# Attention feeding a routed expert layer: three moves in the order of the GpSimd queue

## The chip, the core and the metric

The kernel runs on one core of a Trainium2 chip. The core has a matrix engine (PE in the profile), a vector engine (DVE), an activation engine (ACT), a general engine that also issues descriptor-built DMAs (POOL, GpSimd) and an engine that only synchronises and issues DMAs (SP). The metric is the device time of one execution in microseconds. Before the change it is 408.72 us, the median of 3 runs (408.39 to 409.97).

## The reference

```python
def _attn_ref(q, k, v, w1, b1, w2):              # q, k, v: 8 batches, 8 heads, 576 positions, 64 wide
    scores = q @ k.transpose(0, 1, 3, 2) / sqrt(D)
    x = log1p(|i - j|) / log1p(max(i, 1))         # a distance for each query i and key j
    bias = relu(x[..., None] @ w1 + b1) @ w2      # 32 hidden units, one bias per head
    attn = softmax(scores + bias)
    return attn @ v
def _moe_ref(x, domain_id, w1, w2):               # x: 4608 tokens of 512; 8 experts, hidden 1024
    for e in range(8):
        mask = domain_id == e
        out[mask] = relu(x[mask] @ w1[e]) @ w2[e]
```

The attention output of 8 batches times 576 positions is the 4608 tokens of the expert layer. Each token goes to the one expert that its domain names.

## The kernel before, in words

The kernel has three stages. The first builds the bias table and the routing table (which row of a DRAM buffer, `fire_x`, each token goes to, sorted by expert). The second runs the attention batch by batch and scatters the finished tokens into `fire_x`. The third reads `fire_x` expert by expert, transposed by DMA, runs the two matrix products of each expert, and scatters the rows into the output.

**A batch of attention** has 21 units, written as a list in `run`: the scores of a group of heads and keys are made by PE, exponentiated by ACT, multiplied by the bias on DVE, and multiplied with v by PE. What else is done beside each unit stands in the table `PLAN`, one string per unit, counted from 0 to 20. In it T0 to T3 transpose q and k of the next batch for head pairs 0 to 3 on PE, and T4 transposes the last 64 queries and keys of the next batch (the tile `last`); D0 to D4 copy the results to SBUF on DVE; A makes the product with v, N divides by the sums; a mark ' means the batch before. T4 stands in unit 1, T0 in unit 3, T3 in unit 15. N4' (the last 64 queries of the batch before, which land in the tile `xl`) stands in unit 3 and N3' (its last head pair, which completes the tile `xt`) in unit 7. PE, DVE and ACT run in exactly the written order, so a transpose that waits for its load holds up everything behind it on PE.

**Tokens out.** `xt` holds 512 positions of a batch in four column blocks, `xl` the other 64. Half of each `xl` row is computed on the wrong partitions, so SP copies it over (L686) before it can be scattered. A batch leaves by five indirect DMAs on POOL (L698): one for `xl`, four for `xt`.

**Loads.** q, k and v are cast from float32 to float16 on the way, by DMAs on POOL: `load_qk` (L504) brings 512 positions of q and k, `load_last` (L512) the last 64 of both in four small DMAs, `load_v` (L519) and `load_vrag` (L526) v. Each of them is for two batches ahead. q, k and v share six buffers (`n4`), so a load waits until an older tile has been read.

**Order on POOL.** The class `_Issue` chains POOL's DMAs: an ordinary one stands behind everything before it, while a run of scatters may be reordered among itself by the scheduler. POOL executes in order. Every POOL DMA also uses one of eight semaphores in turn, so it waits until the eighth DMA before it has landed.

**Into the expert layer.** Expert 0's first 512 rows are known to come from batches 0 to 6 (`EARLY`), so SP reads them transposed (tile `xA`, L983) as soon as batch 6 is scattered, during batch 7. The other rows of expert 0 and those of experts 1 to 7 are read (tile `xT`, L826) when batch 7 is scattered too. Expert weights come in quarters of 512 KB (L781), 32 in all. On PE, L847 is the first product on `xA`, L855 the one on the rest of expert 0's rows, L837 that of the other experts, L813 the second product. Two second products of expert 0 stand between L847 and L855.

Of the kernel before, what the change touches and what calls it, by code (L numbers as in the profile page):

```python
# [10 lines left out]
F16 = mybir.dt.float16  # L11
# [5 lines left out]
P = 128  # L17
# [3 lines left out]
B = 8  # L21
# [8 lines left out]
EARLY = 512  # L30
# [430 lines left out]
class _Attention:  # L461
# [197 lines left out]
    def norm(self, b, p, halves=(0, 1)):  # L659
        nc, asb = self.nc, self.G.asb  # L660
        pv = self.pu[:, :, 0:260].rearrange("p a (g d) -> p a g d", d=65)
        if p < 4:
            rz = asb.tile([P, 2, 4, 1], F32, tag="rz", name="rz", bufs=2)
            if p == 0:
                self.xt[b] = self.new_rows("xt", P, 4, S * b, 4)
                self.xl[b] = self.new_rows("xl", P, 1, S * b + 512, 1)
            a0, n = halves[0], len(halves)
            a = slice(a0, a0 + n)
            nc.vector.reciprocal(out=rz[:, a], in_=pv[:, a, :, 64:65])
            nc.vector.tensor_tensor(  # L670
                out=self.xt[b][:, 2 * a0: 2 * a0 + 2 * n, 128 * p: 128 * p + 128]
                .rearrange("p (a c) (g d) -> p a c g d", a=n, d=64),
                in0=pv[:, a, :, 0:64].rearrange("p a (c g) d -> p a c g d", g=2),
                in1=rz[:, a].rearrange("p a (c g) d -> p a c g d", g=2).to_broadcast([P, n, 2, 2, 64]),
                op=AO.mult)
            if p == 3:
                for t in range(2 * a0, 2 * a0 + 2 * n):
                    self.scatter(b, t, self.xt[b][:, t, :], 128)
        else:
            rz = asb.tile([P, 2, 4, 1], F32, tag="rz", name="rz", bufs=2)  # L680
            xl = self.xl[b]
            pl = pv[:, 0]
            nc.vector.reciprocal(out=rz[:, 0], in_=pl[:, :, 64:65])
            nc.vector.tensor_tensor(out=xl[:, 0, 0:256].rearrange("p (g d) -> p g d", d=64), in0=pl[:, :, 0:64],  # L684
                                    in1=rz[:, 0].to_broadcast([P, 4, 64]), op=AO.mult)
            nc.sync.dma_start(out=xl[0:64, 0, 256:DM], in_=xl[64:128, 0, 0:256])  # L686
            self.scatter(b, 4, xl[0:64, 0, :], 64)

    def new_rows(self, tag, n, c, base, step):

# [22 lines left out]
    def run(self, late):  # L713
        units = [("r", 0)] + [("m", p, c) for p in (0, 1) for c in range(4)] + [("r", 1)] + \
                [("m", 2, c) for c in range(4)] + [("l", 0), ("l", 1), ("x",)] + \
                [("m", 3, c) for c in range(4)]
        NU = len(units)
        self.joined = {("l", 0): 0, ("l", 1): 1}
        for p in range(4):
            n = 4 if all(2 * p < RAW.get(c, H) for c in range(4)) else 2  # L720
            self.joined.update({("m", p, c): c % 2 for c in range(n)})
        jobs = {}

        def act(what, b, n):
            if what[0] in "TD":
                if b + 1 < B:
                    (self.transposes if what[0] == "T" else self.take)(b + 1, int(what[1]))
            elif b < 0 or b >= B:
                pass
            elif what[0] == "V":  # L730
                self.make_vext(b)
            elif what[0] == "W":
                self.weight(jobs.pop((b, int(what[1:]))))
            elif what[0] == "A":
                p, c = int(what[1]), int(what[2])
                if c == 0:
                    self.av_begin(b, p)
                self.av(b, p, c)
                if (b, p) == (B - 1, 3) and c % 2 == 1:
                    self.norm(b, p, (c // 2,))  # L740
            elif what[0] == "N" and (b, int(what[1])) != (B - 1, 3):
                self.norm(b, int(what[1]))

        def plan(b, ui):

            if b < B - 1:
                return PLAN[ui].split()
            if b == B:
                return [w for w in PLAN[ui].split() if w[:2] not in ("A4", "N4")]
            return {19: "W16 N2 A40 A41", 20: "A42 A43 W18 N4"}.get(ui, PLAN[ui]).split()  # L750

        for n in range((B + 1) * NU):
            b, ui = divmod(n, NU)
            if b < B:
                jobs[b, ui] = self.scores(b, units[ui])
            if (b, ui) == (0, 5):
                self.nc.vector.memset(self.vx[1][:, :, :, 64:65], 1.0)
            if b == 0 and ui in (1, 2):
                self.transposes(0, 1 + ui)
                self.take(0, 1 + ui)  # L760
            if b < B - 2 and ui == 8:
                self.load_last(b + 2)
                self.load_qk(b + 2)
            if b < B - 2 and ui == 10:
                self.load_v(b + 2)
                self.load_vrag(b + 2)
            late(b, ui)
            for what in plan(b, ui):
                act(what.rstrip("'"), b - what.count("'"), n)
# [152 lines left out]
def kernel(  # L922
# [13 lines left out]
    nc = tc.nc  # L936
    G = _Ctx()
# [10 lines left out]
    with tc.manual_schedule(engines={ET.PE, ET.DVE, ET.Activation}):  # L948
        with ExitStack() as att:
            G.asb = att.enter_context(tc.tile_pool(name="asb", bufs=1))  # L950
            G.biasM = G.asb.tile([P, 4, H, 512], F16, tag="biasM", name="biasM")
            G.biasW = {c: G.asb.tile([P, H - h, 512], F16, tag=f"biasW{c}", name=f"biasW{c}")
                       for c, h in RAW.items()}
            G.biasR = G.asb.tile([P, 4, 512], F16, tag="biasR", name="biasR")
            G.biasL = G.asb.tile([P, 2, 2, 2, 4, 64], F16, tag="biasL", name="biasL")
            G.biasRL = G.asb.tile([P, 4, 64], F16, tag="biasRL", name="biasRL")
            G.zero = G.asb.tile([P, 4, XW], F16, tag="xt", name="zero", bufs=2)
            G.dom2 = G.pbuf.tile([P, B, NT, 2], I32, tag="dom2", name="dom2")
            nc.vector.memset(G.dom2[:, :, 4, :], 99)
            with tc.tile_pool(name="tmp", bufs=1, side="right") as G.tmp:  # L960
                _setup_constants(tc, G, w1, b1, w2)
            wsb = ctx.enter_context(tc.tile_pool(name="wsb", bufs=1, side="right", reuse_waits="tile"))
            G.w_first = lambda name: wsb.tile([P, 2048], F16, tag="w", name=name, bufs=11)
            dom2 = _load_domains(tc, G, moe_domain_id)
            route = _phase_route(tc, G, dom2, x_dram)
            next(route)
            at = _Attention(tc, G, q, k, v, x_dram)
            at.start()
            _phase_bias(tc, G, route, at, x_dram)
            with tc.tile_pool(name="aps", bufs=1, space=PS, reuse_waits="tile") as G.aps:  # L970
                def late(b, ui):
                    if (b, ui) == (0, 2):
                        G.w.load(2, G.w_first)
                        _clear_overflow(tc, G, x_dram)
                    if (b, ui) == (6, 8):
                        G.w.load(3, G.n4)
                        G.w.load(2, G.w_first)
                    if (b, ui) == (7, 11):
                        G.w.load(2, G.n4)
                        G.w.load(2, G.w_first)  # L980
                    if (b, ui) == (B - 1, 9):
                        G.early = G.n4("xA").rearrange("p (c t) -> p c t", c=4)
                        nc.sync.dma_start_transpose(out=G.early, in_=x_dram[0: EARLY, 0:DM])  # L983
                at.run(late)
        G.msb = ctx.enter_context(tc.tile_pool(name="msb", bufs=1, reuse_waits="tile"))
        wsb2 = ctx.enter_context(tc.tile_pool(name="wsb2", bufs=1, reuse_waits="tile"))
        G.w_late = lambda name: wsb2.tile([P, 2048], F16, tag="w", name=name, bufs=12)
        G.mps = ctx.enter_context(tc.tile_pool(name="mps", bufs=1, space=PS, reuse_waits="tile"))
        _phase_moe(tc, G, moe_w1, moe_w2, x_dram, out)
# [31 lines left out]
```

## Time and profile before

| | |
|---|---|
| median of 3 runs | 408.72 us |
| the profiled execution, and its span | 408.06 us, 406.5 us |
| attention batches (from 55.6 us on) | to 245.5 us |
| expert layer | from 245.5 us to the end |
| PE busy, ACT busy, DVE busy, POOL busy | 334.1, 250.9, 235.1, 186.6 us |
| mean granted TensorE clock | 0.908 |

Times in the views are counted from the start of the span. A timeline row gives start, length, engine, line, operation, out<-in and count; a bracket at its end gives how long the engine stood idle before it, and what ended the wait. A row of the waits view gives who waited for whom, the total, how often, and the longest.

### The profile page before, as it was taken

The numbers are of one execution on the slowest core, as the hardware profiler recorded it, in microseconds if no ns is written. First come the engines' busy times: TensorE is split into PE (matmuls) and PEld (weight loads), VectorE is DVE, ScalarE is ACT, GpSimd is POOL, SyncE is SP. The second block draws the span as 40 slices with busy tenths as digits, with TensorE's granted clock in tenths as the row PEclk, the third lists the DMA queues.
The fourth block names the chain that finished last, engine by engine and source line by source line (L and its number), as shares of the span: only waits on it lengthen the run. The fifth ranks groups of instructions, "written<-read, shape, count | busy, mean of one in ns | idle before, by whom it ended". The sixth has DMA issues, their size and how long they took to land. (4 is left out here: it accounts for less than half of the span.)

```text
span 406.5 us, 9749 instructions
## 1 busy us (share of the span) xinstructions
PE 334.1 (82%) x4098; PEld 215.8 (53%) x4098; DVE 235.1 (58%) x450; ACT 250.9 (62%) x306; POOL 186.6 (46%) x228
## 2 busy tenths in 40 slices
PE   1588778989496996969789870899999999999990
PEld 1477754656274563737456550356565564655640
DVE  7999998999488694968959872020302213021220
ACT  8999976999497794969869970225142241513310
POOL 9250307729266491836637180422627354141331
PEclk9999566999799796998979996699999999999996
DMA  5999980874919569392965949389999999930211
GB/s 92 175 205 371 236 140 3 94 93 72 167 48 128 79 87 139 64 160 57 122 90 113 198 86 203 88 165 227 195 235 225 228 209 239 248 118 27 99 72 49
DMA packets 87668, 57.37 MB, mean 141 GB/s; under 512 B 44741, under 2 KB 78789, under 8 KB 87624
## 3 DMA queue, kind: packets, MB, share of 16 engines
q0 software_dynamic: 56960, 45.13, 64.6%
q1 hardware_dynamic: 30664, 11.62, 13.9%
q8 instruction: 32, 0.52, 0.5%
q14 instruction: 12, 0.10, 0.1%
HBM read 61.93 MB, written 24.70 MB: 213 GB/s over the span
## 5 line engine op out<-in xcount | busy, mean ns | idle before, releaser
L613 ACT ACTIVATE e<-sc 128x1024 f16<-128x1024 f32 x160 | 152.2, 1048 | 33.2 <-PE sc L587 31.9
L816 DVE COPY res<-ops 128x512 f32<-128x512 f32 x40 | 27.7, 692 | 121.9 <-PE ops L813 120.9
L873 ACT ACTIVATE hT<-hps 128x640 f16<-128x640 f32 x56 | 39.4, 704 | 78.1 <-PE hps L837 78.1
L624 DVE TENSOR_TENSOR e<-e,biasM 128x2048 f16<-128x2048 f16 x64 | 73.3, 1154 | 8.7 <-ACT e L613 8.3
L817 POOL DMA_INDIRECT out_dram<-res,ids x40 | 39.5, 987 | 78.4 <-DVE res L816 65.5
L813 PE MATMUL ops<-w,hT 128*128 128x512 f16 x320 | 70.5, 379 | 0.0
L837 PE MATMUL hps<-xT,w 128*128 128x320 f16 x448 | 62.0, 299 | 0.0
L698 POOL DMA_INDIRECT fire_x<-xt,posi x32 | 43.0, 1343 | 33.1 <-DMA xl<-xl 13.8
L587 PE MATMUL sc<-qkT 64*128 64x512 f16 x256 | 54.1, 417 | 4.8 <-ACT e L613 3.6
L837 PEld LDWEIGHTS <-w 128*128 128x128 f16 x448 | 43.7, 98 | 18.2
L641 PE MATMUL pu<-vext,e 128*128 128x65 f16 x1024 | 53.0, 202 | 0.3 <-DVE e L624 0.3
L813 PEld LDWEIGHTS <-hT 128*128 128x128 f16 x320 | 31.1, 98 | 36.5 <-ACT hT L849 0.3
L641 PEld LDWEIGHTS <-e 128*128 128x128 f16 x1024 | 47.0, 103 | 2.2 <-issue 0.8
L698 POOL DMA_INDIRECT fire_x<-xl,posi x8 | 10.7, 1338 | 55.6 <-DMA xl<-xl 45.6
L781 POOL DMA_DIRECT2D w<-in_moe_w_dram x32 | 25.8, 819 | 21.2 <-DMA vst<-in_v_dram 9.3
L240 PE MATMUL eb<-W2BIG,e 128*128 128x32 f16 x432 | 19.9, 193 | 16.0 <-DVE e L223 10.7
L559 DVE COPY qkT<-pt 128x1024 f16<-128x1024 f16 x32 | 21.9, 684 | 16.8 <-PE pt L534 16.7
L637 PE MATMUL pu<-vrag,e 128*128 128x130 f16 x128 | 30.0, 234 | 1.5 <-DVE xl L684 0.8
L223 DVE TENSOR_SCALAR e<-L,slope,nb 128x576 f16<-128x576 f16 x86 | 31.2, 433 | 0.0
L240 PEld LDWEIGHTS <-e 128*128 128x128 f16 x432 | 17.7, 117 | 18.2 <-DVE e L223 11.2
L534 PE MATMUL pt<-idn,kn 128*64 128x128 f16 x256 | 15.0, 246 | 13.6 <-DMA kn<-in_k_dram 13.6
L587 PEld LDWEIGHTS <-qkT 64*128 64x128 f16 x256 | 14.5, 94 | 21.1 <-issue 12.7
(144 smaller groups left out, 407.5 us busy)
## 6 DMA issues: line engine op xcount, KB each, us to landing
w<-in_moe_w_dram POOLq DMA_DIRECT2D x32, 512.0 KB, 12.7
fire_x<-zero SPq DMA_DIRECT2D x1, 5140.0 KB
qn<-in_q_dram POOLq DMA_DIRECT2D x8, 512.0 KB, 6.3
kn<-in_k_dram POOLq DMA_DIRECT2D x8, 512.0 KB, 8.5
vst<-in_v_dram POOLq DMA_DIRECT2D x8, 512.0 KB, 10.7
out_dram<-res,ids POOLq DMA_INDIRECT x40, 6.5
last<-zero SPq DMA_DIRECT2D x2, 256.0 KB, 3.0
last<-in_q_dram POOLq DMA_DIRECT2D x16, 32.0 KB, 2.4
```

What stands on the lines that cost most here:

```text
L223: nc.vector.tensor_scalar(out=hr, in0=G.L4[:, c0: c0 + S], scalar1=G.slope[:, m: m + 1], scalar2=G.nb1[:], op0=AO.mult, op1=AO.max)
L240: nc.tensor.matmul(out=eb[:, lj, 32 * k16: 32 * k16 + 32], lhsT=hr[:, jc: jc + 4 * 127 + 1: 4], rhs=G.W2BIG[:, 0:32], start=True, stop=True)
L587: mm(out=sc[:, h2, :], lhsT=self.qkT[b, p][hs[h2], 1, 128 * c: 128 * c + 128], rhs=self.qkT[b, p][hs[h2], 0, :], start=not raw, stop=True)
L613: nc.scalar.activation(out=ef[:, 0:n], in_=sf[:, 0:n], func=AF.Exp, bias=0.0, scale=0.125)
L624: self.nc.vector.tensor_tensor(out=job[0], in0=job[0], in1=job[1], op=AO.mult)
L637: mm(out=self.pu[:, c // 2, o: o + 130], lhsT=er[:, p % 2, 128 * c: 128 * c + 128], rhs=vr[:, p, :], start=True, stop=False, skip_group_ch ...
L641: mm(out=self.pu[:, c // 2, o + 65 * h2: o + 65 * h2 + 65], lhsT=self.e[b, ("m", p, j)][:, h2, 128 * c: 128 * c + 128], rhs=vx[:, 2 * p + ...
L698: inst = self.nc.gpsimd.indirect_dma_start(out=self.x_dram[:, :], out_offset=bass.IndirectOffsetOnAxis(ap=self.G.posi[0:n, c:c + 1], axis= ...
L813: nc.tensor.matmul(out=ops_, lhsT=hT[:, fc, t0: t0 + 128], rhs=G.w.w2(e, fc), start=(fc == 0), stop=(fc == 7))
L817: inst = nc.gpsimd.indirect_dma_start(out=out[:], out_offset=bass.IndirectOffsetOnAxis(ap=idx.bitcast(I32), axis=0), in_=res[:], in_offset ...
L837: nc.tensor.matmul(out=hps[:, i, 0:HC], lhsT=G.w.w1(e, dc)[:, 128 * fc: 128 * fc + 128], rhs=xT[:, dc, HC * hf: HC * hf + HC], start=(dc = ...
L873: nc.scalar.activation(out=hT[:, fc, :].rearrange("p (a b) -> p a b", a=2), in_=first(e, xT, ((fc, 0), (fc, 1))), func=AF.Relu, bias=0.0, ...
```

## The change

Three edits, and small companions of them. First, the scatter of `xl` is written behind those of `xt`. Second, `load_qk` for two batches ahead moves from unit 8 to unit 2, in front of the scatters of the batch before; `load_v` and `load_vrag` move from unit 10 to unit 8; in batch 0 the transposes of its own pairs 2 and 3, which free the buffers, move from units 1 and 2 to units 2 and 6, with their copies to units 3 and 7. Third, four weight quarters that were loaded in unit 11 of batch 7 are issued behind the read of `xA`, and behind a small POOL copy of one column of `xA`, which can't run before `xA` has landed.

```diff
@@ norm
             if p == 3:
                 for t in range(2 * a0, 2 * a0 + 2 * n):
                     self.scatter(b, t, self.xt[b][:, t, :], 128)
+                if b in self.xl:
+                    self.scatter(b, 4, self.xl.pop(b)[0:64, 0, :], 64)
         else:
...
             nc.sync.dma_start(out=xl[0:64, 0, 256:DM], in_=xl[64:128, 0, 0:256])
-            self.scatter(b, 4, xl[0:64, 0, :], 64)
@@ run
-            if b == 0 and ui in (1, 2):
-                self.transposes(0, 1 + ui)
-                self.take(0, 1 + ui)
+            if b == 0 and ui in (2, 6):
+                self.transposes(0, 2 + ui // 6)
+            if b == 0 and ui in (3, 7):
+                self.take(0, 2 + ui // 7)
+            if b < B - 2 and ui == 2:
+                self.load_qk(b + 2)
             if b < B - 2 and ui == 8:
                 self.load_last(b + 2)
-                self.load_qk(b + 2)
-            if b < B - 2 and ui == 10:
                 self.load_v(b + 2)
                 self.load_vrag(b + 2)
@@ the kernel's late()
-                    if (b, ui) == (7, 11):
-                        G.w.load(2, G.n4)
-                        G.w.load(2, G.w_first)
                     if (b, ui) == (B - 1, 9):
                         G.early = G.n4("xA").rearrange("p (c t) -> p c t", c=4)
                         nc.sync.dma_start_transpose(out=G.early, in_=x_dram[0: EARLY, 0:DM])
+                        seen = G.pbuf.tile([P, 1], F16, tag="seen", name="seen")
+                        G.issue(nc.gpsimd.tensor_copy(out=seen, in_=G.early[:, 3, EARLY - 1: EARLY]))
+                        G.w.load(2, G.n4)
+                        G.w.load(2, G.w_first)
```

POOL's queue in a middle batch (the scatters are those of the batch before, the loads those for two ahead; L698, L781 and L817 of the kernel before are L700, L784 and L820 of the changed one), before:

```order
L698 DMA fire_x<-xl,posi 9216x514
L698 DMA fire_x<-xt,posi 9216x514 x4
L512 DMA last_159<-in_q_dram 64x4x64 x2
L512 DMA last_159<-in_k_dram 64x4x64 x2
L504 DMA qn<-in_q_dram 128x8x256
L504 DMA kn<-in_k_dram 128x8x256
L519 DMA vst<-in_v_dram 128x8x256
L526 DMA vrag_150<-in_v_dram 64x4x64 x2
L692 IOTA xt 128x4
L692 IOTA xl 128x1
```

and now:

```order
L694 IOTA xt 128x4
L694 IOTA xl 128x1
L504 DMA qn<-in_q_dram 128x8x256
L504 DMA kn<-in_k_dram 128x8x256
L700 DMA fire_x<-xl,posi 9216x514
L700 DMA fire_x<-xt,posi 9216x514 x4
L512 DMA last_159<-in_q_dram 64x4x64 x2
L512 DMA last_159<-in_k_dram 64x4x64 x2
L519 DMA vst<-in_v_dram 128x8x256
L526 DMA vrag_150<-in_v_dram 64x4x64 x2
```

q and k stand in front of the five scatters, `last` still behind them. The scatter of `xl` is still the first of the five: the scheduler is free to order them, and it leaves `xl` in front in batches 0 to 6.

POOL's queue in batch 0, now (`pi` is the table of rows to clear, L433 the eight clears of overflow rows, w the weight quarters; before, q and k of batch 2 stood behind `last_158`):

```order
L416 IOTA pi 128x8
L504 DMA qn<-in_q_dram 128x8x256
L504 DMA kn<-in_k_dram 128x8x256
L784 DMA w_1370<-in_moe_w_dram 128x4x512
L784 DMA w_1372<-in_moe_w_dram 128x2x1024
L433 DMA fire_x<-zero,pi 2304x2056 x8
L512 DMA last_158<-in_q_dram 64x4x64 x2
L512 DMA last_158<-in_k_dram 64x4x64 x2
L519 DMA vst<-in_v_dram 128x8x256
```

Two weight quarters, the eight clears and `last` of batch 2 now stand behind q and k of batch 2. In the changed program k of batch 2 waits for the buffer that held q of batch 0, which the transposes of pair 3 read in unit 6.

POOL's queue at the end of the attention, now:

```order
L986 COPY seen<-xA 128x1
L784 DMA w_4565<-in_moe_w_dram 128x4x512
L784 DMA w_4567<-in_moe_w_dram 128x4x512
L784 DMA w_4569<-in_moe_w_dram 128x2x1024
L784 DMA w_4571<-in_moe_w_dram 128x2x1024
L694 IOTA xt 128x4
L694 IOTA xl 128x1
L700 DMA fire_x<-xt,posi 9216x514 x2
L700 DMA fire_x<-xl,posi 9216x514
L700 DMA fire_x<-xt,posi 9216x514 x2
```

The copy is new; the four loads and the scatters of batch 7 stood in the same order before, with `xl` second among the scatters, where it is now third.

## The prediction

> **What bounds the kernel now.** I read the view of waits first, for PE, because PE, ACT and DVE run in a written order and whatever PE waits for stops all three.
>
> ```profile
> PE pt L534 <- DMA kn<-in_k_dram: 13.6, 6, 3.2
> ...
> PE hps L847 <- DMA xA<-fire_x: 10.3, 1, 10.3
> ...
> PE pt L534 <- DMA qn<-in_q_dram: 7.8, 5, 2.4
> ```
>
> Three loads stop PE: k and q of the next batch, 21.4 us together, and expert 0's first rows, 10.3 us. The timeline of PE shows where. These are the T4 transposes of batches 1, 2 and 6 (ptl), two waits for k, and the first scores of batches 2 and 7 (L593).
>
> ```profile
> 81.00 0.62 PE L534 MATMUL ptl<-idn,last 128*128 128x128 f16 x8
> ...
> 84.15 0.41 PE L534 MATMUL pt<-idn,kn 128*64 128x128 f16 x8 [0.92 <-DMA kn<-in_k_dram]
> ...
> 99.30 0.59 PE L593 MATMUL sc<-qkT,qkTl 128*128 128x512 f16 x2 [0.17 <-ACT e L613]
> ...
> 100.59 0.62 PE L534 MATMUL ptl<-idn,last 128*128 128x128 f16 x8
> ...
> 108.51 0.64 PE L534 MATMUL pt<-idn,kn 128*64 128x128 f16 x8 [3.21 <-DMA kn<-in_k_dram]
> ...
> 198.70 0.62 PE L534 MATMUL ptl<-idn,last 128*128 128x128 f16 x8
> ...
> 221.72 0.59 PE L593 MATMUL sc<-qkT,qkTl 128*128 128x512 f16 x2 [0.17 <-ACT e L613]
> ```
>
> From T4 to T4, batch 1 takes 100.59 - 81.00 = 19.59 us with hardly a wait. The next four take (198.70 - 100.59) / 4 = 24.53 us each. The difference, 4.9 us a batch, is the wait for q and k and its aftermath. Why q and k are late stands in the timelines of POOL and SP.
>
> ```profile
> 83.63 0.50 SPq L686 DMA_DIRECT2D xl<-xl  x1
> ...
> 103.21 0.47 SPq L686 DMA_DIRECT2D xl<-xl  x1
> ```
> ```profile
> 88.29 1.78 POOL L698 DMA_INDIRECT fire_x<-xl,posi  x1 [9.67 <-DVE xt L670]
> ...
> 96.32 1.34 POOL L512 DMA_DIRECT2D last<-in_q_dram  x2
> 97.61 1.27 POOL L512 DMA_DIRECT2D last<-in_k_dram  x2
> 98.81 0.98 POOL L504 DMA_DIRECT2D qn<-in_q_dram  x1
> 99.70 0.98 POOL L504 DMA_DIRECT2D kn<-in_k_dram  x1
> ...
> 109.29 0.97 POOL L698 DMA_INDIRECT fire_x<-xl,posi  x1 [5.86 <-DMA xl<-xl]
> ```
>
> It is a loop through POOL: the copy of `xl` lands, five scatters go, then four small loads of `last`, then q and k, which batch 2 wants at once. k is issued at 99.70 and used at 108.51.
>
> **The change part by part. q and k in front.** In a middle batch they now stand ahead of the scatters. POOL reaches them as soon as the previous batch's loads are out, a whole batch before T0 wants them. They cannot be what T0 waits for. The 24.53 us loop is gone, and the question is what is late next. `last` is: it stays behind the scatters and is wanted by T4, two units earlier than T0. The new loop starts from T4:
>
> - T4 to the issue of the `xl` copy: 83.63 - 81.00 = 2.63 us.
> - The copy until POOL's first scatter: 88.29 - 83.63 = 4.66 us in batch 1, where only v was still loading, and 109.29 - 103.21 = 6.08 us in batch 2, with q, k and v on the way. From now on q, k and v are always on the way then (they go out just before), so I take 6.08.
> - Five scatters: 96.32 - 88.29 = 8.03 us. Four loads of `last`: 97.61 + 1.27 - 96.32 = 2.56 us.
> - Their landing: T4 of batch 2 ran at 100.59, so at most 1.71 us behind 98.88.
>
> The sum is 21.0 us. With 4.66 for the copy it is 19.6, just what batch 1 took: in batch 1 the loads of `last` land at the very moment T4 wants them, so they have no slack to lose. Hence 21.0 us a batch from T4 of batch 1 to T4 of batch 6, with a wait of about 1.4 us at each T4. Bounds: 19.6 with the quick copy; 22 if the short waits also slow PE down. For that, the same timeline after two more waits for k:
>
> ```profile
> 132.99 0.64 PE L534 MATMUL pt<-idn,kn 128*64 128x128 f16 x8 [2.05 <-DMA kn<-in_k_dram]
> ...
> 180.93 0.41 PE L534 MATMUL pt<-idn,kn 128*64 128x128 f16 x8 [2.24 <-DMA kn<-in_k_dram]
> ```
>
> Eight transposes take 0.41 us at the full clock and 0.64 slowed. After 0.92 us of waiting (84.15) and after 2.24 us (180.93) they were quick, after 2.05 us slow. One wait of 1.4 us is nearer to the quick ones, so I add nothing, and because of the slow group I keep 22 as a bound. The Trainium skill, page "TensorE: Matmul & The Clock Gate", Part 1, says the clock falls only after an idle window of about 3.4 us. By that rule there would be no bound of 22; the slow group behind 2.05 us does not agree with it.
>
> **The price at the start.** k of batch 2 now waits in POOL's queue for the transposes of unit 6 of batch 0. Behind it stand two weight quarters, eight clears and `last` of batch 2. The rows are PE's scores of unit 6, the clears as a group, the loads of `last` behind them, and four weight loads issued in a row, with their landing:
>
> ```profile
> 65.47 0.61 PE L587 MATMUL sc<-qkT 64*128 64x512 f16 x2 [0.69 <-ACT e L613]
> ```
> ```profile
> L433 POOL DMA_INDIRECT fire_x<-zero,pi x8: 959/992/1466, 61.0 to 70.9; - x8
> ```
> ```profile
> 71.87 1.35 POOL L512 DMA_DIRECT2D last<-in_q_dram  x2
> ```
> ```profile
> L781 POOL DMA_DIRECT2D w<-in_moe_w_dram x4: 761/802/831, 239.5 to 241.8; - x4
> ...
> DMA to landing us min/median/max: 6.1/8.9/11.1
> ```
>
> The q half of the transposes ends about 0.7 us after 65.47, at 66.2. Then k 1.0, two weights 1.6, the clears 71.87 - 61.0 = 10.9, `last` 2.6 and its landing 1.7: T4 of batch 1 at 84.0 instead of 81.0. That costs 3 us (0, if PE reaches unit 6 three us sooner; 5, if the clears wait for the landing of the weights, which the eight semaphores can make them do). What the moved transposes spare PE in batch 0 only lengthens this wait, so it counts nothing.
>
> So T4 of batch 6 comes at 84.0 + 5 x 21.0 = 189.0. No q, k or `last` is loaded for batch 8, so from there batch 7's first scores follow as in batch 1: 99.30 - 81.00 = 18.3, less 0.7 for its own wait, 17.6. That is 206.6 against 221.72: **15.1 us gained**.
>
> **`xl` behind `xt`.** In batches 0 to 6 the scheduler leaves `xl` in front, and in batch 7 it goes from second to third of five, all of which the next read waits for. Nothing, either way.
>
> **x of expert 0 alone.** PE, SP and POOL around the end of the attention, then the read of expert 1's 640 rows:
>
> ```profile
> 245.05 0.22 PE L637 MATMUL pu<-vrag,e 128*128 128x130 f16 x1
> ...
> 255.85 9.18 PE L847 MATMUL hps<-xA,w 128*128 128x512 f16 x32 [10.33 <-DMA xA<-fire_x]
> 264.87 3.62 PE L813 MATMUL ops<-w,hT 128*128 128x512 f16 x16
> 268.32 1.95 PE L855 MATMUL hps<-xT,w 128*128 128x128 f16 x32
> ```
> ```profile
> 241.30 10.16 SPq L983 DMA_TRANSPOSE xA<-fire_x  x1
> ...
> 264.35 1.20 SPq L826 DMA_TRANSPOSE xT<-fire_x  x1
> ```
> ```profile
> 256.63 1.04 POOL L698 DMA_INDIRECT fire_x<-xt,posi  x1 [13.84 <-DMA xl<-xl]
> ```
> ```profile
> L826 SPq DMA_TRANSPOSE xT<-fire_x x1: 2749/2749/2749, 266.2 to 266.2; - x1
> ...
> DMA to landing us min/median/max: 4.8/4.8/4.8
> ```
>
> Counted from batch 7's first scores (221.72), `xA` is issued at 19.6 and PE is done at 23.8. Beside four weight loads the read took 14.5 us. Alone it should take no more than the 4.8 us of the larger read, so it lands at 24.4 and L847's wait shrinks from 10.3 to 0.6 us. Before, the four weights had landed at 241.8 + 11.1 = 252.9, ahead of batch 7's first scatter, which the read of `xA` held back until 256.63. Now they start only with the landing of `xA`, right in front of those scatters. They are in the same DMA queue, which the landing times of loads issued just behind each other show to be served in order:
>
> ```profile
> vst<-in_v_dram POOLq DMA_DIRECT2D x8, 512.0 KB, 10.7
> ...
> vrag<-in_v_dram POOLq DMA_DIRECT2D x16, 32.0 KB, 9.6
> ```
>
> A `vrag` of 32 KB takes as long as the `vst` in front of it. The first weight lands 6.1 us after its issue, and the last at 241.8 + 11.1 - 239.5 = 13.4 us after the first's issue, so 2.4 us apart. From the landing of `xA`: weights landed at 0.3 + 13.4 = 13.7; four and a half scatters of a quarter of their bytes behind them, 0.6 us each (an estimate from the 2.4), 16.4; expert 0's other rows read and used, at most 268.32 - 264.35 = 4.0 and I take 3.0: L855 at 19.4. PE is ready at 7.2 + 3.6 = 10.8 (32 products at the pace of the 16 of L813). So PE waits 8.6 us in front of L855: **most of the wait moves from L847 to L855**. L855 comes at 24.4 + 19.4 = 43.8 after batch 7's start, where it was 268.32 - 221.72 = 46.6: 2.8 us gained. Before, the slow restart (9.18 against 7.2 us) lay in front of L855, now it lies behind: 1.9 lost. Net 0.9. Bounds: +4.8 if the scatters aren't held, -2 if the scatters' bytes take twice as long.
>
> From L855 on PE runs through to the end as before. The sum: 15.1 + 0.9 = 16.0 us off the profiled execution's 408.06, so 392; its time lies 0.7 below the median of the runs, so 393 for these.
>
> **The rivals.** *Free batches:* the `xl` copy stays as quick as in batch 1 and `last` is just in time, 19.6 a batch, 5 x 1.4 = 7 us more: 386. For it, batch 1; against it, five later copies that took about 6 us. *Scatters not held:* 4 to 5 us more: 388. *Slower than before:* the `xl` copy is drowned. q, k and v are now all queued in the same microseconds as the copy, and each us on it costs five, one in each of five batches. From 6.1 + (16 + 2) / 5 = 9.7 us on, the kernel is slower; at 10 it takes 412. Against it, the copy of batch 6, issued behind five weight quarters of 512 KB:
>
> ```profile
> 225.19 0.46 SPq L686 DMA_DIRECT2D xl<-xl  x1
> ```
> ```profile
> 231.68 1.27 POOL L698 DMA_INDIRECT fire_x<-xl,posi  x1 [10.25 <-DMA xl<-xl]
> ```
>
> 6.5 us, hardly more than with q, k and v. The Trainium skill, "DMA: Bandwidth & Descriptors", section "Queues, rings and completion order", gives a reason: each DMA engine takes turns between the queues it has work for, packet by packet, so a small copy on SP's queue doesn't stand behind POOL's backlog. By that rule this rival falls away; the 6.5 agrees. *The edit doesn't do what it says* holds for `xl` behind `xt`, and is in the sum.
>
> **How the numbers follow.** The forecast's own mechanism, 388 to 399, 0.55; free batches or unheld scatters, below 388, 0.22; a costlier start or slowed PE, 399 to 406.7, 0.10; within 0.5% (about what a measurement of this kernel can tell from no change), 0.06; the drowned copy, slower, 0.07. Faster by over 0.5%: 0.87. The range 384 to 403 leaves a little under 2 in 10 outside.
>
> **What would show it.** Right: no PE wait for qn or kn in batches 1 to 6; short waits of ptl for `last`, 3 us or more in batch 1 and 1 to 2 us behind; T4 to T4 about 21; copy to scatter about 6; L847 hardly waiting, and 8 to 9 us of waiting in front of L855. Wrong: batches at 19.6 with no wait for `last` (the copy was mis-sized), L855 without a wait (the queue isn't in order), or T4 to T4 above 23.

## The result and the profile after

The changed kernel takes 389.13 us (median, 388.91 to 390.09) where the kernel before took 409.35 us beside it (408.39 to 410.63): ratio 0.9509, 95% interval 0.9475 to 0.9543. Forecast were 393 us and a range of 384 to 403. The profiled execution took 389.06 us, its span is 387.1 us (406.5 before), and the granted clock is 0.971 on average (0.908 before). In the comparisons further down some executions, the traced one with `last` moved in batches 1 to 5 among them, were several per cent slower than the others of their kernel; the times given are medians of all, the ratios leave these out.

Line numbers have moved by two or three: L698 is now L700, L686 is L689, L781 is L784, L847 is L850, L855 is L858, L813 is L816, L826 is L829. The view of waits for PE in the changed kernel, each row with the total, the count and the longest wait:

```profile
PE hps L858 <- DMA xT<-fire_x: 7.7, 1, 7.7
PE ptl L534 <- DMA last<-in_k_dram: 5.6, 6, 1.5
...
PE ptl L534 <- DMA last<-in_q_dram: 3.4, 4, 1.6
```

The 13.6 and 7.8 us for `kn` and `qn` are gone, and the 10.3 us for `xA` have shrunk to 0.37. New are 9.0 us for `last`, in small pieces in front of T4, and 7.7 us for expert 0's other rows, in front of L858. The timeline of PE has the T4 transposes of batches 1 (the q half, then the k half), 2 (k half) and 6 (k half), and the first scores of batch 7:

```profile
83.30 0.38 PE L534 MATMUL ptl<-idn,last 128*128 128x128 f16 x4 [1.33 <-DMA last<-in_q_dram]
84.60 0.45 PE L534 MATMUL ptl<-idn,last 128*128 128x128 f16 x4 [0.91 <-DMA last<-in_k_dram]
...
106.07 0.38 PE L534 MATMUL ptl<-idn,last 128*128 128x128 f16 x4 [1.51 <-DMA last<-in_k_dram]
...
186.16 0.38 PE L534 MATMUL ptl<-idn,last 128*128 128x128 f16 x4 [0.77 <-DMA last<-in_k_dram]
...
204.27 0.59 PE L593 MATMUL sc<-qkT,qkTl 128*128 128x512 f16 x2 [0.17 <-ACT e L613]
```

Five batches take (186.16 - 84.60) / 5 = 20.31 us each from T4 to T4, where four took 24.53. Batch 7 begins at 204.27 instead of 221.72: 17.45 us earlier.

The end of the attention, on PE, POOL and SP:

```profile
228.44 8.59 PE L850 MATMUL hps<-xA,w 128*128 128x512 f16 x32 [0.37 <-DMA xA<-fire_x]
236.87 3.62 PE L816 MATMUL ops<-w,hT 128*128 128x512 f16 x16
248.15 3.59 PE L858 MATMUL hps<-xT,w 128*128 128x128 f16 x32 [7.66 <-DMA xT<-fire_x]
```
```profile
228.46 0.19 POOL L986 COPY seen<-xA 128x1 f16<-128x1 f16 x1 [6.38 <-DMA xA<-fire_x]
228.96 3.00 POOL L784 DMA_DIRECT2D w<-in_moe_w_dram  x4 [0.32 <-issue]
...
232.41 1.06 POOL L700 DMA_INDIRECT fire_x<-xt,posi  x1 [0.20 <-POOL xl L694]
...
237.59 0.97 POOL L700 DMA_INDIRECT fire_x<-xt,posi  x1 [0.30 <-issue]
```
```profile
224.08 2.22 SPq L983 DMA_TRANSPOSE xA<-fire_x  x1
...
245.31 1.21 SPq L829 DMA_TRANSPOSE xT<-fire_x  x1
```

The read of `xA`, alone now, lands 228.44 - 224.08 = 4.4 us after its issue, where it took 14.5 before. The four weight quarters go out behind it, the scatters behind them. The last scatter's issue ends at 238.56, but the read of `xT`, which waits until the scatters have landed, is issued at 245.31. So L858 comes 43.88 us after batch 7's first scores. Before, L855 came 46.60 us after them. From there to the end of the span it is 138.95 us (138.18 before).

The whole difference of the spans is thus 17.45 + 2.72 - 0.77 = 19.4 us. Nine tenths of it come from the attention.

### The profile page after: what moved, and what is told of

Same layout as the page of the kernel before. It is cut to its first block, busy times and chain, and to the rows that moved or that the text cites. A ratio compares the mean times of both kernels' runs of the same rounds, so it can differ in the third digit from the quotient of the medians.

```text
span 387.1 us, 9750 instructions
## 1 busy us (share of the span) xinstructions
PE 331.2 (86%) x4098; PEld 214.7 (55%) x4098; DVE 235.9 (61%) x450; ACT 250.1 (65%) x306; POOL 177.0 (46%) x229
## 5 line engine op out<-in xcount | busy, mean ns | idle before, releaser
L820 POOL DMA_INDIRECT out_dram<-res,ids x40 | 39.7, 993 | 71.8 <-DVE res L819 53.1
L816 PE MATMUL ops<-w,hT 128*128 128x512 f16 x320 | 70.8, 380 | 0.0
L840 PE MATMUL hps<-xT,w 128*128 128x320 f16 x448 | 62.0, 299 | 0.0
L587 PE MATMUL sc<-qkT 64*128 64x512 f16 x256 | 52.9, 408 | 4.2 <-ACT e L613 3.3
L840 PEld LDWEIGHTS <-w 128*128 128x128 f16 x448 | 43.8, 98 | 18.1
L816 PEld LDWEIGHTS <-hT 128*128 128x128 f16 x320 | 31.3, 98 | 36.6 <-ACT hT L852 0.3
L641 PE MATMUL pu<-vext,e 128*128 128x65 f16 x1024 | 49.8, 196 | 0.3 <-DVE e L624 0.3
L641 PEld LDWEIGHTS <-e 128*128 128x128 f16 x1024 | 44.0, 99 | 2.4 <-issue 1.1
L700 POOL DMA_INDIRECT fire_x<-xt,posi x32 | 35.7, 1114 | 9.6 <-issue 7.9
L784 POOL DMA_DIRECT2D w<-in_moe_w_dram x32 | 25.0, 791 | 30.5 <-ACT biasR L253 10.4
L240 PE MATMUL eb<-W2BIG,e 128*128 128x32 f16 x432 | 19.7, 194 | 15.7 <-DVE e L223 9.5
L700 POOL DMA_INDIRECT fire_x<-xl,posi x8 | 9.0, 1125 | 50.9 <-DVE rz L669 41.7
L637 PE MATMUL pu<-vrag,e 128*128 128x130 f16 x128 | 29.1, 227 | 1.5 <-DVE xl L687 0.8
L240 PEld LDWEIGHTS <-e 128*128 128x128 f16 x432 | 17.5, 117 | 17.9 <-DVE e L223 11.1
L670 DVE TENSOR_TENSOR xt<-pu,rz 128x512 f16<-128x512 f32 (+1 forms) x33 | 22.3, 675 | 1.5
```

Of the source, the lines that this page charges most:

```text
L240: nc.tensor.matmul(out=eb[:, lj, 32 * k16: 32 * k16 + 32], lhsT=hr[:, jc: jc + 4 * 127 + 1: 4], rhs=G.W2BIG[:, 0:32], start=True, stop=True)
L587: mm(out=sc[:, h2, :], lhsT=self.qkT[b, p][hs[h2], 1, 128 * c: 128 * c + 128], rhs=self.qkT[b, p][hs[h2], 0, :], start=not raw, stop=True)
L637: mm(out=self.pu[:, c // 2, o: o + 130], lhsT=er[:, p % 2, 128 * c: 128 * c + 128], rhs=vr[:, p, :], start=True, stop=False, skip_group_ch ...
L641: mm(out=self.pu[:, c // 2, o + 65 * h2: o + 65 * h2 + 65], lhsT=self.e[b, ("m", p, j)][:, h2, 128 * c: 128 * c + 128], rhs=vx[:, 2 * p + ...
L700: inst = self.nc.gpsimd.indirect_dma_start(out=self.x_dram[:, :], out_offset=bass.IndirectOffsetOnAxis(ap=self.G.posi[0:n, c:c + 1], axis= ...
L816: nc.tensor.matmul(out=ops_, lhsT=hT[:, fc, t0: t0 + 128], rhs=G.w.w2(e, fc), start=(fc == 0), stop=(fc == 7))
```

## The experiments

All times of one group are from one chip, beside runs of the kernel before there.

### The third and the first edit undone

The weights of the third edit back in unit 11 of batch 7, in front of the read of `xA`:

```diff
+                    if (b, ui) == (7, 11):
+                        G.w.load(2, G.n4)
+                        G.w.load(2, G.w_first)
...
-                        seen = G.pbuf.tile([P, 1], F16, tag="seen", name="seen")
-                        G.issue(nc.gpsimd.tensor_copy(out=seen, in_=G.early[:, 3, EARLY - 1: EARLY]))
-                        G.w.load(2, G.n4)
-                        G.w.load(2, G.w_first)
```

> The changed kernel with its third edit undone: the four weight quarters go out in unit 11 of batch 7 again, beside the read of xA, and there is no POOL copy. Theory (the wait in front of the first product on xA has only moved to the product on expert 0's rest): batch 7 starts at about 204 as in the changed kernel, PE then waits about 10 us for xA and not at all in front of the product on the rest, which comes 46.6 us after batch 7's start in place of 43.9, with PE already warm: 2.7 - 0.8 = 1.9 us slower than the changed kernel, about 391. Rival (the third edit is worth the whole 10 us that left the first product): about 399.

Measured: 390.69 us, ratio 0.9509 (0.9405 to 0.9613), the same ratio as the changed kernel's above; the interval, about 4 us to each side, is too wide to tell the 1.9 us expected. In its view of waits the wait for `xA` is back and the one for `xT` is gone:

```profile
PE hps L850 <- DMA xA<-fire_x: 10.7, 1, 10.7
```
```profile
250.63 1.95 PE L858 MATMUL hps<-xT,w 128*128 128x128 f16 x32
```

L858 comes 46.56 us after batch 7's first scores (204.07), as expected (46.6). The third edit moves a wait and is worth next to nothing by itself: 10.7 us in one place against 0.4 + 7.7 in two, and 387.7 us of span against 387.1.

The scatter of `xl` back at its old place in the code:

```diff
-                if b in self.xl:
-                    self.scatter(b, 4, self.xl.pop(b)[0:64, 0, :], 64)
...
             nc.sync.dma_start(out=xl[0:64, 0, 256:DM], in_=xl[64:128, 0, 0:256])
+            self.scatter(b, 4, xl[0:64, 0, :], 64)
```

> The changed kernel with its first edit undone: the scatter of xl written ahead of those of xt. Only batch 7's order differs: xl second of five, not third. Theory: no difference, 389 within 1 us, same waits. Rival (waiting for the copy of xl in POOL holds up two scatters of batch 7 and with them expert 0's rest): 390 to 392.

Measured: 388.29 us, ratio 0.9416 (0.9351 to 0.9481), waits of 9.1 us for `last` and 7.9 us for `xT`. Nothing that can be told from the changed kernel, as expected. So, by exclusion, the second edit makes practically the whole gain, together with its companions (the transposes of batch 0, the earlier v), which no run took apart. The waits agree: those for `kn` and `qn`, which it aimed at, are the ones that are gone.

### `last` in front of the scatters too

If the new loop runs through the scatters to `last`, the waits of T4 must go when `last` goes out with q and k. Two doses: in batches 1 to 5 only, and in all.

```diff
             if b < B - 2 and ui == 2:
                 self.load_qk(b + 2)
+                self.load_last(b + 2)
             if b < B - 2 and ui == 8:
-                self.load_last(b + 2)
                 self.load_v(b + 2)
```

The smaller dose (with `if b > 0` before the added line, and `last` in unit 8 still in batch 0):

> The changed kernel, and the four loads of last go out right behind q and k, in front of the scatters, in batches 1 to 5 (batch 0 as it is). Theory (the new loop runs through last): no wait of the T4 transposes in batches 2 to 6, 19.6 us from T4 to T4 in place of 20.3, so 5 x 0.7 = 3.4 us faster than the changed kernel, about 385.7; the wait of batch 1 stays. Rival (the waits come from full DMA rings, not from last's place in the queue): the waits stay or move to another load, 388 to 390.

Measured: 383.05 us, ratio 0.9341 (0.9302 to 0.9379), 2.7 us better than expected. In its trace `last` is waited for in batch 1 alone (1.4 and 0.9 us), as expected, and from T4 of batch 2 to that of batch 6 a batch takes 18.86 us, not 19.6. In all batches:

> As the kernel before, and in batch 0 too, where last of batch 2 then stands in front of two weight quarters and the eight clears. Theory: T4 of batch 1 at about 81.9 in place of 84.6 with no wait, so another 2.5 us: about 383. Rival (something else in batch 1 is late too, such as q and k of batch 3): as the kernel before, about 386.

Measured: 378.98 us, ratio 0.9239 (0.9170 to 0.9309); again on another chip, below, 378.34. No wait for `last` is left in either trace. The timeline of PE on that other chip, with T4 of batches 1 and 2 in one piece each:

```profile
81.89 0.62 PE L534 MATMUL ptl<-idn,last 128*128 128x128 f16 x8
...
100.73 0.62 PE L534 MATMUL ptl<-idn,last 128*128 128x128 f16 x8
```

So T4 of batch 1 is back near 81.0, and a batch takes 18.84 us (in the first of the two traces 80.77 and 18.84). The loop through `last` is what was left, and it cost more than forecast: the prediction held 19.59 us for a free batch, but that batch 1 of the kernel before had a wait of its own, the 0.92 us for `kn` at 84.15, in it. What paces a batch now is ACT. These are its exponentials from 80 to 205 us in the changed kernel and in the first of the two traces (busy time, mean ns, idle time before them):

```profile
L613 ACT ACTIVATE e<-sc 128x1024 f16<-128x1024 f32 x122 | 115.2, 1061 | 9.9 <-PE sc L587 9.5
```
```profile
L613 ACT ACTIVATE e<-sc 128x1024 f16<-128x1024 f32 x134 | 125.0, 1062 | 0.4
```

ACT's idle time has gone from 9.9 to 0.4 us, so moving loads further ahead can gain hardly anything more in these batches.

### The weights at the end of the attention

The theory: the queue is served in order, so the scatters of batch 7 land behind the weights issued in front of them. Then the wait in front of L858 falls with each quarter that goes behind the scatters. Two quarters behind them:

```diff
                         seen = ...
                         G.w.load(2, G.n4)
-                        G.w.load(2, G.w_first)
...
                 at.run(late)
+                G.w.load(2, G.w_first)
```

> The changed kernel with two of the four weight quarters in front of batch 7's scatters and two behind them. Theory (scatters are served behind the quarters, 2.4 us each): expert 0's rest is 4.9 us less late, the wait in front of its product falls from 7.7 to about 2.8 us, 5 us faster in the profiled time. Rival (the scatters are slow for another reason, such as the copy of xl): the wait stays at 7 to 8 us.

and all four:

> The changed kernel with all four weight quarters behind batch 7's scatters. Theory: scatters landed about 9.5 us after xA, expert 0's rest used at 12.4, PE ready at 12: wait 0 to 1 us, so 7 us and the slow restart gained, 381 to 382, unless the quarters now delay the reads of expert 0's rest and expert 1, as they delayed xA in the kernel before; then 2 to 5 us of it come back as a wait in front of one of these, 384 to 387. Rival (queue order does not matter): 389.

Both missed. PE waited 7.5 us for `xT` with two quarters behind, and 8.3 us with four; the times were 402.83 us (one run) and 406.28 us (ratio 0.9848, 0.9741 to 0.9954; more on these times below). The rivals' figures (7 to 8 us of waiting, no gain) came closer, but not for their reason. The timelines show why. Two quarters behind: POOL's last scatter, the issue of the read, and L858, which starts when the read has landed:

```profile
250.07 0.98 POOL L700 DMA_INDIRECT fire_x<-xt,posi  x1 [0.30 <-issue]
```
```profile
256.07 1.27 SPq L829 DMA_TRANSPOSE xT<-fire_x  x1
```
```profile
261.86 3.59 PE L858 MATMUL hps<-xT,w 128*128 128x128 f16 x32 [7.54 <-DMA xT<-fire_x]
```

Four behind, the same three:

```profile
245.64 0.97 POOL L700 DMA_INDIRECT fire_x<-xt,posi  x1 [0.30 <-issue]
```
```profile
248.39 2.39 SPq L829 DMA_TRANSPOSE xT<-fire_x  x1
```
```profile
259.74 3.21 PE L858 MATMUL hps<-xT,w 128*128 128x128 f16 x32 [8.29 <-DMA xT<-fire_x]
```

| weights in front of, behind the scatters | last scatter's end to issue of `xT` | issue of `xT` to L858 | both |
|---|---|---|---|
| 4, 0 (the change) | 6.75 | 2.84 | 9.6 |
| 2, 2 | 5.02 | 5.79 | 10.8 |
| 0, 4 | 1.78 | 11.35 | 13.1 |

The first column does what the theory says: fewer weights in front, and the scatters land sooner. Counted from the small copy (L986) that marks the landing of `xA`, at 228.46, 242.35 and 239.79, the read goes out after 16.9, 13.7 and 8.6 us: 8.3 us for four quarters, 2.1 each, where the prediction took 2.4. But the read of `xT` then runs beside the weights behind it, and loses there more than the scatters gained. The read of `xA` beside four weights had taken 14.5 us in the kernel before; the first expectation forgot that the same holds for `xT`, and the second named it, with 2 to 5 us, where the wait was 8.3. So the weights must be neither in front of the scatters nor beside the read. Issued behind expert 0's scatters of results:

```diff
                         seen = ...
-                        G.w.load(2, G.n4)
-                        G.w.load(2, G.w_first)
...
+            if (e, kk) == (0, NCH - 1):
+                G.w.load(2, G.n4)
+                G.w.load(2, G.w_first)
             if e > 0 or kk == NCH - 1:
```

> The changed kernel with the four quarters behind the output scatters of expert 0's fourth block. Theory: as the kernel before without the collision with the reads: the wait in front of expert 0's rest gone, none in front of expert 1, 381 to 382. Against it: later quarters might be missed by expert 2 or 3, which would show as PE waiting for w.

The wait for `xT` fell to 1.1 us, now in front of L840, and none is left in front of L858. PE waited for no weights. The time was 401.12 us (397.18 to 415.07), with no ratio given. With `last` in front of all scatters as well:

> last in front of the scatters in all batches, and the four quarters behind expert 0's output scatters. Theory: the two gains add up, 6 + 7 us: about 376. Rival (with the attention shorter or the quarters later, the weights or the DMA rings become what the experts wait for): 379 or more, with waits for w.

394.10 us, ratio 0.9573 (0.9483 to 0.9662). The wait for `xT` was down to 0.7 us in front of L858 and 1.4 in front of L840, and yet both were slower than expected: in the profiles of all four kernels on this chip batch 7's first scores came at 215 to 222 us, 11 to 18 us later than in the changed kernel's profile, though moving the weights leaves the program of the attention alone. Whether the chip or the edit did that had to be told apart.

### Four kernels on one chip

The changed kernel unaltered:

> The changed kernel unaltered, beside the three others on one chip, because the comparisons with the weights moved ran on another chip than it and their attention stage was slower there although its program was the same. Theory A (that chip): it repeats 389 us here, ratio 0.951, with a wait of 7.7 us for xT in front of the first expert's second half, if this chip is like the first; on a chip like the second, it too has its seventh batch's last-query products at 213 to 223 us instead of 204.3, and 397 to 406 us. Theory B (moving the weights itself slows attention, by where the pools come to lie): 389 us with 204.3 here while the kernels with moved weights have 213 to 223.

the later weights alone:

> Four quarters of weights issued behind expert 0's scatters of results, so that nothing of 512 KB is in flight beside the last scatters and the read of xT. From the products on xA to the end it took 149.1 us on the second chip, against 158.7 in the changed kernel on the first, so theory A expects the changed kernel's time of this chip less 8 to 10 us (380 beside 389), no wait of over 1.5 us for xT. Theory B: 397 to 401 us beside 389.

`last` in front alone:

> Last queries' loads in front of the scatters in all batches. Theory A: the changed kernel's time of this chip less 10 us (379 beside 389), no wait for last; the wait for xT stays at 8 to 9 us, because the weights are still in front of the last scatters. Rival: on a chip whose attention is slower for another reason, the gain is smaller, 4 us or less, since last is then not what is waited for.

and both:

> Both: theory A adds the two, since one takes waits of batches 1 to 6 and the other the one behind batch 7: 18 to 20 us below the changed kernel (370 beside 389). Rival 1: the gain of the first is lost in the second (the later weights become the bound of the experts once these start earlier): 375 to 380. Theory B: 391 to 394 us beside 389.

Measured, with the kernel before at 410.04 us (408.48 to 411.85) there:

| kernel | us | ratio | batch 7's first scores | L850 | L858 | span |
|---|---|---|---|---|---|---|
| changed | 387.25 | 0.9422 (0.9358 to 0.9487) | 202.21 | 226.25 | 246.72 | 385.5 |
| later weights | 379.70 | 0.9235 (0.9171 to 0.9299) | 201.57 | 226.16 | 239.44 | 378.0 |
| `last` in front | 378.34 | 0.9216 (0.9157 to 0.9274) | 193.76 | 218.85 | 238.13 | 377.1 |
| both | 376.51 | none given | 192.89 | 216.74 | 228.54 | 366.1 |

Theory B falls: with the weights later, batch 7 starts where it does in the changed kernel, so the edit doesn't slow the attention, and L858 comes 7.3 us sooner. That leaves theory A, the chip or the hour; the changed kernel never ran on the other chip, so what slowed the attention there is not shown. The three rows of the later weights again, POOL, SP, PE:

```profile
232.10 0.97 POOL L700 DMA_INDIRECT fire_x<-xt,posi  x1 [0.31 <-issue]
```
```profile
234.66 1.21 SPq L829 DMA_TRANSPOSE xT<-fire_x  x1
```
```profile
239.44 1.95 PE L858 MATMUL hps<-xT,w 128*128 128x128 f16 x32
```

The read goes out 1.6 us after the last scatter, and L858 follows on L816 without a wait, at full pace (1.95 us, against 3.59 behind the wait). `last` in front gains 8.4 us by batch 7's first scores. In the profile of both, the gains stand one behind the other, 385.5 - 366.1 = 19.4 us of span against 7.5 and 8.4 alone (the sum is 15.9). Against `last` in front alone it is 11.0 us: 7.5 from L850 to L858, 0.9 in the attention (193.76 - 192.89), 1.2 from there to L850, where `last` in front alone waited 1.3 us for `xA`, and 1.4 behind L858, from where the span's end is 137.56 us away with both and 138.97 with `last` in front alone. The last three make up the 3.5 us beyond the sum; each is a difference of two single traces, and that the edits make it isn't shown. The rows of both:

```profile
216.74 8.51 PE L850 MATMUL hps<-xA,w 128*128 128x512 f16 x32
225.09 3.62 PE L816 MATMUL ops<-w,hT 128*128 128x512 f16 x16
228.54 1.95 PE L858 MATMUL hps<-xT,w 128*128 128x128 f16 x32
```

Its four times fall into two pairs, 367.96 and 370.37, 382.65 and 382.82; 376.51 is the median of all four. The lower pair would be 0.90 of the kernel before, 17 to 19 us below the changed kernel's median, about what theory A asked. The median lies where the rival put it, but the wait for weights by which the rival explained it isn't in the trace of the first run. Even the slower pair is below the changed kernel, so this version beats both kernels. What separates the pairs was not found: only the first was profiled.

## Why the prediction was right

**The loop that replaces the old one.** Right in kind: nothing waits for q or k, `last` is late at each T4, by 0.9 to 2.3 us. In batch 1 it was 2.2 us, where the prediction asked for 3 or more. The pace was 20.31 us a batch, forecast 21.0. That these lie so close is partly luck: two terms of the sum were mis-sized, against each other. Batch 1's loop, on SP (the copies of `xl` of batches 1 and 2) and POOL:

```profile
86.99 0.50 SPq L689 DMA_DIRECT2D xl<-xl  x1
...
107.92 0.47 SPq L689 DMA_DIRECT2D xl<-xl  x1
```
```profile
94.67 0.97 POOL L700 DMA_INDIRECT fire_x<-xl,posi  x1 [7.63 <-DVE rz L669]
...
100.08 0.97 POOL L700 DMA_INDIRECT fire_x<-xt,posi  x1 [0.30 <-DMA fire_x<-xt,posi]
101.05 1.35 POOL L512 DMA_DIRECT2D last<-in_q_dram  x2
102.36 1.26 POOL L512 DMA_DIRECT2D last<-in_k_dram  x2
```

| term | forecast | T4 of batch 1 to 2 | T4 of batch 2 to 3 |
|---|---|---|---|
| T4 to the copy | 2.63 | 2.39 | 1.85 |
| copy to first scatter | 6.08 | 7.68 | 7.35 |
| five scatters | 8.03 | 6.38 | 6.10 |
| four loads of `last` | 2.56 | 2.57 | 2.57 |
| landing, to T4's k half | 1.71 | 2.45 | 1.79 |
| sum | 21.0 | 21.47 | 19.66 |

The copy was under-sized by 1.3 to 1.6 us here, and by 0.8 to 1.4 in the three batches that follow: the step took 6.08 from a batch with q, k and v on the way, but the copy itself now lands later. The groups of its six issues from 84 to 205 us, changed kernel first, then the kernel before:

```profile
L689 SPq DMA_DIRECT2D xl<-xl x6: 461/462/498, 87.0 to 188.1; - x6
...
DMA to landing us min/median/max: 4.1/6.5/6.9
```
```profile
L686 SPq DMA_DIRECT2D xl<-xl x6: 461/462/497, 83.6 to 201.4; - x6
...
DMA to landing us min/median/max: 3.8/5.2/5.3
```

The scatters were over-sized by 1.7 to 1.9 us. The step took 8.03 from batch 1 of the kernel before, as if a scatter's issue had a fixed price. It hasn't. Minimum, median and maximum in ns of the scatters of `xt`, changed kernel, then before:

```profile
L700 POOL DMA_INDIRECT fire_x<-xt,posi x24: 965/996/1977, 95.9 to 200.3; - x24
```
```profile
L698 POOL DMA_INDIRECT fire_x<-xt,posi x20: 993/1407/1737, 90.4 to 191.7; - x20
```

The rival *free batches*, 386 us, came close in three of the five batches (19.7 us), though not by its own way: the copy was slower, not as quick as in batch 1, and `last` was waited for. Nor was its 19.6 us the floor that it was taken for, as the 18.84 us above show.

**The start.** k of batch 2 went out at 66.55 (forecast 66.2), the eight clears took 69.19 to 80.20, 11.0 us (10.9), and T4 of batch 1 came at 84.60, with its k half (84.0). From T4 of batch 6 to batch 7's first scores it took 18.11 (17.6). With the pace 5 x 0.69 = 3.45 us better and these two 1.1 worse, batch 7 came 2.3 us before the forecast of 206.6.

**`xl` behind `xt`** is worth nothing, as said, and undoing it showed that.

**The tail.** The most exact step in its sum. Landing of `xA` 24.2 us after batch 7's first scores (24.4), wait there 0.37 (0.6), L858 19.7 us behind it (19.4), wait in front of it 7.66 (8.6), L858 43.88 us after batch 7's first scores (43.8). The scatters are held by the weights in front of them; the table of doses shows that. The read of `xT` went out 16.9 us after the landing of `xA` (16.4). Mis-sized was PE's own way to L858: L850 was to take 7.2 us once its long wait was gone, and took 8.59 behind a wait of 0.37, at a granted clock of 0.82. So PE was ready 12.05 us after L850's start, not 10.8, and the wait was the shorter for it, which cost nothing. The slow restart behind the wait was sized rightly: L858 took 3.59 us at a clock of 0.50, and from its start to POOL's last output scatter (268.32 to 397.75 before, 248.15 to 379.42 now) 1.84 us were lost (1.9). Not in the forecast was that the span ends 1.1 us sooner behind that scatter, 6.7 us in place of 7.8; that is luck, and leaves 0.77 of the loss.

**The sum.** Forecast 16.0 us; measured 19.4 us of span, 2.3 more from the attention and 1.1 more from the tail. The likeliest case was the one that came; the 4 us between 393 and 389 are mostly the pace and the quicker end.

**The drowned copy** did not come: with all three big loads around it, the copy to the first scatter took 6.9 to 7.7 us in batches 1 to 5, under the 9.7 from which the kernel would have been slower, though nearer to it than the 6.08 taken. That agrees with the rule of the Trainium skill that the prediction weighed there ("DMA: Bandwidth & Descriptors", section "Queues, rings and completion order"), by which each DMA engine takes turns between the queues it has work for. Taking turns isn't being free of the others: the median landing of the copy rose from 5.2 to 6.5 us.

**The clock.** The prediction added nothing for a slowed PE, because eight transposes behind most short waits were quick. But the speed of the one group behind a wait doesn't show whether the clock fell. In the changed kernel the four transposes of the k half took 0.45 us at 84.60, behind waits of 1.33 and 0.91 us, and the granted clock then stood at 0.50 until 88.2; it did so again from 187.2 to 190.6, behind the waits of batch 6 (1.56 and 0.77 us), and nowhere else between 79 and 219 us. In the kernel before there were five such stretches, of 3.4 or 6.8 us each, and with `last` in front in all batches (the first of its two traces) there is none. What they cost was not measured apart. The group behind 2.05 us from which the prediction took its bound of 22 is one of these, and the clock had fallen ahead of that wait, behind another 1.64 us:

```profile
130.35 0.58 PE L534 MATMUL pt<-idn,qn 128*64 128x128 f16 x8 [1.64 <-DMA qn<-in_q_dram]
...
132.99 0.64 PE L534 MATMUL pt<-idn,kn 128*64 128x128 f16 x8 [2.05 <-DMA kn<-in_k_dram]
```

In the changed kernel's repeat on the other chip one wait was longer, and the four transposes behind it took 0.59:

```profile
84.79 0.59 PE L534 MATMUL ptl<-idn,last 128*128 128x128 f16 x4 [3.56 <-DMA last<-in_q_dram]
```

Behind 3.60 us (the later weights on that chip) and 3.66 us (`xl` undone), though, the four took 0.38 and 0.39, and the next four, behind another 0.73 and 0.62 us, 0.58. The Trainium skill's idle window of about 3.4 us ("TensorE: Matmul & The Clock Gate", Part 1), held against the length of a single wait as in the prediction, does not fit these rows: the clock fell behind shorter waits and was still full behind longer ones.

## What to carry to other kernels

When a load that an engine waits for is moved ahead, follow the queue it left: whatever still stands behind the old obstacle is the next thing to be late, and moving it along too (here the small loads of `last`) was worth another 9 us beside the 23 on one chip. A bulk load costs at the place where it is in flight beside something urgent: in front of scatters in its own queue it delays their landing, behind them it delays the read that follows, so it has to go where neither is near. A scatter's issue and a small copy don't keep the price they had at their old place (here the copy was up to 1.6 us off, the five scatters up to 1.9), so a sum made of old rows is no surer than that. And see whether the "free" stretch that serves as a floor really has no wait in it.

## What the runs showed of the hardware that had not been expected

The same scatter's issue takes 0.97 us or up to 2.0 us on POOL. In the changed kernel the median one took 0.996, before 1.407. Why stays open; no run here was made to test it. The row of batch 1's first scatter names DVE's reciprocal (L669) as what released it, but that doesn't show that POOL waits for DVE: the scatter starts 0.8 us behind the landing of the copy (86.99 + 6.9 = 93.9, then 94.67), and so it does in the kernel before where the row names the copy itself (103.21 + 5.3 = 108.5, then 109.29).

The read by a transposing DMA took 4.4 us (`xA`, 512 rows) or 2.8 us (`xT` of expert 0, 128 rows) with no weights beside it, 5.8 us (`xT`) where two 512 KB loads had started to go out 5.0 us before it, and 11.4 (`xT`) and 14.5 us (`xA`) where four had started to go out 1.8 us before it.

Two chips, in one session each, differ more in one kernel than in another. The kernel with the later weights took 397.18 us at best on one and 378.44 on another, the kernel before 409.62 and 408.48. ACT's exponentials of the slow one, from 80 to 205 us, then of the quick one (busy time, mean ns, idle time before them):

```profile
L613 ACT ACTIVATE e<-sc 128x1024 f16<-128x1024 f32 x113 | 106.7, 1061 | 19.8 <-PE sc L587 7.3 <-PE pu L641 4.8 <-PE pt L534 3.6
```
```profile
L613 ACT ACTIVATE e<-sc 128x1024 f16<-128x1024 f32 x124 | 116.5, 1065 | 8.7 <-PE sc L587 8.3
```

Each instruction takes as long; the slow one has more pauses. Most of them are waits for PE's products, and PE in turn waits for ACT. One pause of ACT has no cause that the profile shows, and PE's next product waits until ACT is done:

```profile
144.41 1.02 ACT L613 ACTIVATE e<-sc 128x1024 f16<-128x1024 f32 x1 [1.67 <-issue]
```
```profile
145.48 0.61 PE L600 MATMUL sc<-qkTl,qkT 128*128 128x128 f16 x8 [1.58 <-ACT e L613]
```

What starts these pauses stays open. It means that kernels are to be compared on one chip, side by side.
